# One order of work for a conditioned attention and gated-MLP block: mean-root products on either engine, statistics in two tasks, gates in bf16

## The chip, the cores and the metric

The kernel runs on one core of one Trainium2 chip. The core's engines run side by side, each through its own queue of instructions: TensorE (PE) multiplies matrices, with its weight loads shown as PEld, VectorE is DVE, ScalarE is ACT, GpSimd is POOL, and SyncE (SP) issues the transfers. Results of PE land in PSUM, everything else stands in SBUF. The metric is the device time of one execution in microseconds (us); lower is better. A profiled execution gives the trace from which the rows here come. A line such as L753 is a line of the kernel file.

## The reference, cut to what matters

One batch of 2048 tokens of 512 numbers goes through two residual branches. A vector `c` gives six rows that shift, scale and gate the branches.

```python
mod = (silu(c) @ w_mod).reshape(1, 6, 1, 512)
sa, ca, ga, sb, cb, gb = mod[:, 0], ..., mod[:, 5]
h = layernorm(x) * (1 + ca) + sa
x = x + ga * A(h)
h = layernorm(x) * (1 + cb) + sb
x = x + gb * B(h)

def A(h):                       # 32 heads of 16
    q, k, v = split(h @ wqkv)
    pq, pk = q @ w_phi, k @ w_phi           # per head
    phi = lambda p: concat(softmax(p), softmax(-p))
    kv = phi(pk).T @ v;  z = sum over tokens of phi(pk)
    o = (phi(pq) @ kv) / (phi(pq) @ z + 1e-6)
    return o @ wo

def B(h):
    return (sigmoid(h @ w_gate) * (h @ w_up)) @ w_down    # inner width 1376
```

The sums `kv` and `z` run over all tokens. So no output of the attention (no numerator) can be formed before the keys and values of all 2048 tokens are through.

## The kernel before, in words

The 2048 tokens are 16 tiles of 128. The program is first written as a graph of some 1230 small tasks. Each task has a name, the engines it may run on, and the keys that it reads and writes. Then a long string, `ORDER`, lists every task once; the tasks are issued in that order, each to the queue of its engine. `name@A`, `@D` or `@P` puts a task on ACT, DVE or POOL; without a mark it goes to the first engine of its list. Within an engine, tasks run strictly in the order of the string; between engines, semaphores hold a task until what it reads is there. So the string alone decides what waits behind what. It was found by a planner that has a cost in us for each task and engine (the numbers in braces in the code, such as `{"DVE": 0.83}`), but these costs have no part in the running program.

The first stage, up to the first numerators (`num0a`), runs as follows.

- Loads: `ld_x...` bring x in pieces of 2 or 4 tiles, `ld_wk`, `ld_wv` the key and value weights, `ld_wm0...` the first shift and scale weights (two halves, 0 and 1), `ld_wmga` and `ld_wmm2` the other modulation weights, `wqT` transposed query weights, all on SyncE's queue.
- `c1`, `c2`, `c3` form silu(c). `modc1.0`, `modc1.1` multiply it with the first modulation weights, and `modc1c0`, `modc1c1` copy the shift and scale columns out of PSUM (L630 to L638). `modca` and `modc2` do the same for the first gate and for the rest.
- `tpw`, `wTc`, `fold`, `foldc` fold `w_phi` into the key weights (side 1) and query weights (side 0): transposes, copies, products, copies (L661 to L685).
- First layer norm: `st1_t` computes the statistics of tile t and then aggregates them to mean and variance (L702, L703), one task of two DVE instructions. `rs1_g` forms the root of a group of one or two tiles, on ACT (logarithm, exponential, L709) or POOL (L712). `nmr1_g` multiplies mean, root and -1, one small DVE instruction for each tile (L718). `xn1_t` normalizes a tile with root and product as scale and bias (L731; tile 0 on DVE at L729, without the product). `tph` transposes on PE (L744), and `hm1_gj` applies scale and shift to a quarter j of group g, on ACT or DVE (L751, L753). The tiles of groups 6 and 7 (tiles 10 to 13) are transposed by DMA instead (`xT1`).
- Per tile t: `K` and `V` (PE, L817, L821; some in halves a and b), `e` (two exponentials on ACT, L776), `n` (sums on DVE, L780), `r` (reciprocal on DVE, L798, or logarithm and exponential on ACT, L794), `phi` (product on POOL or DVE, L787), `va` (copy of v), and `kv` (PE, accumulates key-value sums, L282). Tiles 11, 13, 14, 15 are cut into parts (`e11.2` is the part from feature group 2).
- For seven query tiles: `Q`, `qe`, `qn`, `qphi`, `pT`, likewise, with the last a transpose by DMA.
- `kvn`, `kvz` mask the finished sums (DVE, L294, L299), and the numerators `num` begin.

The gates: `modcac` and `modc2c` write a gate to four columns of `gcol`. `gwa`, `gwb` store them to DRAM and `gra`, `grb` read them back as a row, spread over all 128 partitions (L843, L846), on SyncE's queue. `wo0` to `wo3` multiply the rows of the output weights by the first gate (L851), `wd0` to `wd10` those of the down weights by the second (L860), on POOL or DVE.

After the numerators the order goes on with division, output product, second layer norm and the MLP (`g`, `tg`, `u`, `hm`, `y`, `fin`, `st`).

```python
def arrange(self, text):
    ...
    for word in text.split():
        name, _, e = word.partition("@")
        t = self.tasks[name]
        t.eng = LETTER[e] if e else next(iter(t.alts))
        assert t.eng in t.alts and t.deps <= done and t not in done, name
...
G.add(f"rs1_{g}", {"ACT": 0.43, "POOL": 1.1}, f_rs, r=[("mv1", t) for t in ts], w=[("rs1", g)])
```

Of the kernel before, what the change touches and what calls it, by code (L numbers as in the profile page):

```python
# [8 lines left out]
FP32 = mybir.dt.float32  # L9
# [3 lines left out]
ALU = mybir.AluOpType  # L13
# [30 lines left out]
K1a hm1_20@A ld_x2a hm1_12 hm1_02@A wqT1 ld_x3a tph03 xn1_4 hm1_23 hm1_13@A tph41 st1_8 hm1_03@A hm1_41@A st1_9 K0a hm1_22@A rs1_6@P tph43 hm1_43@A tph40 K1b
rs1_5@P K0b ld_wv0 wqT3 tph30 tph33 tph32 K2a tph42 hm1_40 wqT2 fold01 hm1_33 tph31 nmr1_6 K2b ld_wmga st1_14 hm1_30@A xn1_11 e0.0 hm1_31@A wqT0 xn1_10 xT1_11
K3a xT1_10 K3b foldc01 nmr1_5 xn1_8 V3a st1_15 e3.0 V0a rs1_8@P e2.0 V0b V3b fold03 va3 foldc03 ld_wmm2 V2a st1_12 n0.0 V2b xn1_9 fold02 nmr1_8 r0.0@A hm1_32
modca.0 va0 foldc02 modca.1 tph50 n2.0 xn1_15 modcac hm1_50 n3.0 e1.0 xn1_14 phi0.0 hm1_60@P V1a V1b hm1_62@P K4a hm1_63@P fold00 tph82 tph52 K4b foldc00
# [113 lines left out]
def kernel(  # L161
# [535 lines left out]
    for g, ts in enumerate(LG):  # L697
        n = len(ts)
        xns = []
        for t in ts:  # L700
            def f_st(e, t=t):
                dve.bn_stats(st1[:, t, :], x_sb[:, t, :])  # L702
                dve.bn_aggr(mv1[:, t, :], st1[:, t, :])  # L703
            G.add(f"st1_{t}", {"DVE": 0.83}, f_st, r=[("x", t)], w=[("mv1", t)])
# [354 lines left out]
```

## Time and profile before

| what | value |
|---|---|
| median of 3 runs | 204.14 us (203.95 to 204.27) |
| the profiled execution | 204.01 us |
| its span, first to last instruction | 202.3 us |
| granted clock of PE | 1.00 |
| busy: PE, DVE, ACT, POOL | 195.3, 160.1, 105.1, 104.7 us |
| moved by DMA | 22.92 MB, mean 113 GB/s |

The span is what the trace covers; the execution's own time lies 1.7 us above it. Busy time counts an instruction from its start to its end; on one engine neighbours can overlap by some hundredths of a us, so a duration may be longer than the room that it takes. In rows of the timeline, "x2" merges neighbours of one kind, and a bracket tells how long the engine stood before the row and what released it. Matmul ends are modelled; their starts are measured.

### The profile page before, as it was taken

What the parts mean: (1) busy time and instruction counts of PE and PEld (TensorE: products, weight loads), DVE (VectorE), ACT (ScalarE), POOL (GpSimd) and SP (SyncE); (2) the same over time, 40 slices, a digit from 0 to 9 for tenths busy, and PEclk for the clock granted to TensorE, in tenths of its full rate; (3) what the DMA queues carried; (4) which work ended last, traced back from release to release, by engine and by line L of the source; (5) the groups of instructions that cost most, each with busy time, mean ns of one, the idle gap of its engine ahead of it and who ended that gap; (6) DMA issues with size and microseconds to landing.
All of it is one profiled execution on the core that took longest, in us unless ns stands there. A gap on an engine that the chain in (4) does not pass through costs nothing.

```text
span 202.3 us, 4156 instructions
## 1 busy us (share of the span) xinstructions
PE 195.3 (97%) x1471; PEld 106.1 (52%) x1471; DVE 160.1 (79%) x374; ACT 105.1 (52%) x253; POOL 104.7 (52%) x147
## 2 busy tenths in 40 slices
PE   7989999999999999999999999999999999999993
PEld 2555565455464787668844444444444444444442
DVE  3999989999999999998897796884969754326623
ACT  2899998999978985576441215212113320334100
POOL 4999987888699998866670066130030332000000
PEclk9999999999999999999999999999999999999999
DMA  5999956669973963418655233542113031000011
GB/s 169 326 293 236 282 213 122 111 57 241 393 281 74 136 103 59 80 34 102 129 78 80 54 76 82 104 105 52 26 26 81 2 78 52 30 3 20 33 55 55
DMA packets 49452, 22.92 MB, mean 113 GB/s; under 512 B 38065, under 2 KB 47634, under 8 KB 49426
## 3 DMA queue, kind: packets, MB, share of 16 engines
q1 hardware_dynamic: 48896, 22.59, 49.7%
q8 instruction: 12, 0.20, 0.4%
q14 instruction: 14, 0.11, 0.2%
q10 hardware_dynamic: 530, 0.02, 0.1%
HBM read 11.58 MB, written 2.10 MB: 68 GB/s over the span
## 4 chain that ended last, share of the span: by engine, by line
PE 74%; DVE 7%; DMA 6%; ACT 5%; SPq 3%; issue 2%; POOL 1%; POOLq 0%; DVEq 0%; ACTq 0%
PE y_ps L485 19%; PE u_ps L447 18%; PE g_ps L447 17%; DMA wmod_sb<-in_w_mod_dram 6%; PE a_ps L356 6%; PE k_ps L817 3%; PE v_ps L821 3%; PE num L326 2%; PE q_ps L871 2%; ACT e L776 2%; DVE ks L780 2%; PE g_ps L449 1%; DVE qks L780 1%; SPq L537 1%; DVE phi L787 1%
## 5 line engine op out<-in xcount | busy, mean ns | idle before, releaser
L457 ACT ACTIVATE tg<-g_ps 128x512 bf16<-128x512 f32 (+5 forms) x66 | 28.9, 455 | 66.8 <-PE g_ps L447 39.7
L485 PE MATMUL y_ps<-wd_sb,wmod_sb 128*128 128x512 bf16 (+4 forms) x187 | 45.7, 367 | 0.0
L468 DVE SCALAR_TENSOR_TENSOR wmod_sb<-tg,u_ps 128x512 bf16<-128x512 bf16 (+4 forms) x63 | 30.3, 491 | 18.0 <-ACT tg L457 11.5
L447 PEld LDWEIGHTS <-wg_sb 128*128 128x128 bf16 (+1 forms) x252 | 21.9, 99 | 16.1
L447 PEld LDWEIGHTS <-wu_sb 128*128 128x128 bf16 (+1 forms) x252 | 21.8, 99 | 15.9 <-issue 0.3
L784 POOL TENSOR_TENSOR qphi<-qe,qks 128x512 bf16<-128x512 bf16 x24 | 25.1, 1061 | 4.2 <-DMA pT<-qphi 1.6
L485 PEld LDWEIGHTS <-wmod_sb 128*128 128x128 bf16 (+1 forms) x187 | 17.0, 97 | 16.0 <-issue 0.6
L447 PE MATMUL u_ps<-wT_sb,wu_sb 128*128 128x512 bf16 (+2 forms) x124 | 23.8, 322 | 0.0
L447 PE MATMUL g_ps<-wT_sb,wg_sb 128*128 128x512 bf16 (+2 forms) x124 | 23.1, 322 | 0.0
L447 PE MATMUL g_ps<-wqk_sb,wg_sb 128*128 128x128 bf16 (+4 forms) x128 | 20.0, 287 | 0.0
L447 PE MATMUL u_ps<-wqk_sb,wu_sb 128*128 128x128 bf16 (+4 forms) x128 | 19.8, 287 | 0.1
L376 POOL TENSOR_SCALAR ve<-mv 128x2 f32<-128x2 f32 (+1 forms) x8 | 1.8, 224 | 33.7 <-DVE mv L366 33.6
L492 DVE TENSOR_TENSOR ot<-y_ps,x 128x512 bf16<-128x512 f32 (+2 forms) x17 | 11.1, 654 | 10.2 <-PE y_ps L485 10.1
L780 DVE TENSOR_REDUCE qks<-qe 128x64 bf16<-128x1024 bf16 x16 | 19.2, 1204 | 0.0
L780 DVE TENSOR_REDUCE ks<-e 128x64 f32<-128x1024 bf16 (+2 forms) x22 | 19.1, 899 | 0.0
L776 ACT ACTIVATE e<-k_ps 128x512 bf16<-128x512 f32 (+2 forms) x44 | 18.0, 514 | 0.0
L776 ACT ACTIVATE qe<-q_ps 128x512 bf16<-128x512 f32 x32 | 17.1, 613 | 0.6 <-POOL phi L787 0.3
L817 PE MATMUL k_ps<-wqk_f,h1T 128*128 128x512 bf16 x64 | 16.6, 379 | 0.0
L871 PE MATMUL q_ps<-wqk_f,h1T 128*128 128x512 bf16 x64 | 15.9, 378 | 0.4 <-ACT wqk_f L685 0.4
L356 PE MATMUL a_ps<-wo_sb,oT 128*128 128x512 bf16 x64 | 16.3, 379 | 0.0
L787 POOL TENSOR_TENSOR phi<-e,kr 128x1024 bf16<-128x1024 bf16 (+2 forms) x10 | 14.4, 1446 | 3.3 <-ACT kr L795 2.1
L821 PE MATMUL v_ps<-wv_sb,h1T 128*128 128x512 bf16 x64 | 15.8, 379 | 0.2 <-ACT vaug L836 0.2
(132 smaller groups left out, 307.4 us busy)
## 6 DMA issues: line engine op xcount, KB each, us to landing
out_dram<-ot SPq DMA_DIRECT2D x15, 128.0 KB, 1.8
x_sb<-in_A_x_dram SPq DMA_DIRECT2D x6, 256.0 KB, 4.7
wmod_sb<-in_w_mod_dram SPq DMA_DIRECT2D x1, 1536.0 KB, 6.9
wu_sb<-in_B_w_up_dram SPq DMA_DIRECT2D x1, 1376.0 KB, 11.3
wg_sb<-in_B_w_gate_dram SPq DMA_DIRECT2D x1, 1376.0 KB, 12.1
wd_sb<-in_B_w_down_dram SPq DMA_DIRECT2D x1, 1280.0 KB, 8.3
wmod_sb<-in_w_mod_dram SPq DMA_DIRECT2D x4, 256.0 KB, 6.1
wqk_sb<-in_A_wqkv_dram SPq DMA_DIRECT2D x2, 256.0 KB, 4.4
```

The costliest lines, as they stand in the source:

```text
L356: pe.matmul(ap_[:], lhsT=oT[:, j, :], rhs=wo_sb[:, j, :], start=(j == 0), stop=(j == KT - 1))
L447: pe.matmul(ps[:fsz, 0:n], lhsT=w[:, j, ft * P:ft * P + fsz], rhs=h[:, j, 0:n], start=(j == 0), stop=(j == KT - 1))
L457: G.add(f"tg{k}.{ft}", {"ACT": 0.13 + n * 0.00083}, lambda e, tg=tg, g_ps=g_ps, fsz=fsz, n=n: act.activation(tg[:fsz, 0:n], g_ps[:fsz, 0:n ...
L468: dve.scalar_tensor_tensor(hm_all[:fsz, hm[k].slot, ft, 0:n], tg[:fsz, 0:n], 1.0, u_ps[:fsz, 0:n], op0=ALU.add, op1=ALU.mult)
L485: mm = pe.matmul(y[:, 0:c1 - c0], lhsT=hm_all[:fsz, hm[k].slot, ft, tl * P:(tl + 1) * P], rhs=wd_sb[:fsz, ft, c0:c1], start=(ft == 0), sto ...
L776: act.activation(ee[:, a:b, s].rearrange("p g f h -> p g (f h)"), kp[:, a * 64:b * 64].rearrange("p (g n) -> p g n", n=64), ACT.Exp, scale ...
L780: dve.tensor_reduce(ks[:, a:b].rearrange("p g s h -> p (g s) h"), ee[:, a:b].rearrange("p g s f h -> p (g s) h f"), axis=AX.X, op=ALU.add)
L784: engine(e).tensor_tensor(ph[:].rearrange("p (g s f h) -> p g s f h", s=2, f=DH, h=4)[:, :, s], ee[:, :, s], ks[:, :, 1 - s].unsqueeze(2). ...
L787: engine(e).tensor_tensor(ph[:, a * P:b * P].rearrange("p (g f h) -> p g f h", f=DH, h=4), ee[:, a:b].rearrange("p g s f h -> p (g s) f h" ...
L817: pe.matmul(kp[:], lhsT=h1T[:, j, t * P:(t + 1) * P], rhs=wqk_f[:, j, D:2 * D], start=(j == 0), stop=(j == KT - 1))
L821: pe.matmul(vp[:], lhsT=h1T[:, j, t * P:(t + 1) * P], rhs=wv_sb[:, j, :], start=(j == 0), stop=(j == KT - 1))
L871: pe.matmul(qp[:], lhsT=h1T[:, j, t * P:(t + 1) * P], rhs=wqk_f[:, j, 0:D], start=(j == 0), stop=(j == KT - 1))
```

## The change: what it does

Three edits in the tasks, and a new order for the first stage. From `num0a` to the end the string is the same, word for word; the sizes, splits and constants are the same too.

1. `nmr1_g` may run on POOL as well as DVE. In the new order all eight (15 instructions) run on POOL.
2. `st1_t` becomes two tasks, `st1s_t` (statistics) and `st1a_t` (aggregate), so that other work can stand between them.
3. The gate columns, their DRAM rows and the spread gate rows are bf16 instead of float32, so the products with `wo` and `wd` read bf16 only, and the spread rows are 1 KB for each partition instead of 2 KB.

Engines that change in the new order (groups and tiles as above):

| from, to | tasks |
|---|---|
| DVE to POOL | nmr1_1 to nmr1_8; qphi2.0, qphi2.1, qphi4.1; phi11.0, phi11.2, phi11.4 |
| ACT to DVE | r1, r2, r3, r4, r6, r9, r10; hm1_00, 03, 10, 11, 20, 21, 30, 31, 42, 82; foldc00; wTc3; modc1c0 |
| DVE to ACT | hm1_12, 23, 32, 40, 50, 52, 81, 83; va2 |
| POOL to DVE | qphi0.0, qphi0.1, qphi1.0, qphi1.1; wo1 |
| POOL to ACT | rs1_0, rs1_4, rs1_6; xn1_7; hm1_60 |

The loads come as x1b, x0a, x0b, wk1, wk0, x1a, x2b, then the four wm0 pieces (before: x0b, x0a, wk0, x1b, wk1, x1a, two wm0 pieces, x2b, two wm0 pieces). The first statistics are of tiles 7, 6, 0, 1, 2, 3, 4, 11, 5, 10 (before: 3, 2, 1, 0, 6, 7, 5, 4). The first key product is of tile 3 (before: tile 1). `mask4`, a small reduction on DVE that `kvn` and `kvz` need, goes to the very start. `gwa`, `gwb` and `gra` stand further ahead of the large weight loads. The diff, cut to its core:

```diff
 ORDER = """
-wdz warm0 c1 warm1_0 warm1_1 warm1_2 warm1_3 warm1_4 ld_x0b st1_3 st1_2 rs1_2 pmem ld_x0a c2 st1_1 ld_wk0 nmr1_2 tpw1 c3 rs1_1 ld_x1b wTc1 nmr1_1 st1_0 ld_wk1
...
+wdz ld_x1b warm0 c1 ld_x0a mask4 pmem c2 bd st1s_7 st1s_6 st1s_0 ld_x0b st1a_7 warm1_0 st1a_6 warm1_1 warm1_2 warm1_3 warm1_4 warm1_5 ld_wk1 warm1_6 rs1_4
+nmr1_4@P warm1_7 st1a_0 rs1_0 st1s_1 xn1_6 tpw2 st1s_2 st1a_1 warm1_8 tpw3 ld_wk0 rs1_1 c3 st1a_2 st1s_3 warm1_9 nmr1_1@P ld_x1a tpw1 tpw0 xn1_1 xn1_7@A tph40
+ld_x2b xn1_0 tph00 st1a_3 wTc3@D wTc2 rs1_2 nmr1_2@P wTc1 fold13 tph11 st1s_4 st1a_4 st1s_11 tph10 ld_wm00b fold11 st1s_5 xn1_3 warm1_10 warm1_11 wTc0 fold10
+st1a_11 foldc13 ld_wm00a xn1_2 st1a_5 foldc11 fold12 ld_wm01a rs1_3@P modc1.0 foldc10 st1s_10 tph41 tph21 modc1c0@D ld_wm01b foldc12 hm1_11 tph23 tph42 hm1_00
+hm1_40@A nmr1_3@P tph20 hm1_10 st1a_10 tph43 hm1_20 hm1_41@A tph01 hm1_01@A hm1_21 ld_x2a modc1.1 tph03 rs1_6 tph22 modc1c1@D hm1_22@A tph02 xn1_4 hm1_03 K3a
...
-    gb_bc = wmod_sb[:].rearrange("p k n -> p (k n)")[:, 2 * FT * 512:].bitcast(FP32)
+    gb_bc = wmod_sb[:].rearrange("p k n -> p (k n)")[:, 2 * FT * 512:2 * FT * 512 + D]
...
-    ga_sb = cst.tile([P, D], FP32, name="ga_sb")
+    ga_sb = cst.tile([P, D], BF16, name="ga_sb")
...
-    gcol = cst.tile([P, 8], FP32, name="gcol")
-    gdr = [drp.tile([P, KT], FP32, name=f"gdr{i}") for i in range(2)]
+    gcol = cst.tile([P, 8], BF16, name="gcol")
+    gdr = [drp.tile([P, KT], BF16, name=f"gdr{i}") for i in range(2)]
...
-            def f_st(e, t=t):
-                dve.bn_stats(st1[:, t, :], x_sb[:, t, :])
-                dve.bn_aggr(mv1[:, t, :], st1[:, t, :])
-            G.add(f"st1_{t}", {"DVE": 0.83}, f_st, r=[("x", t)], w=[("mv1", t)])
+            G.add(f"st1s_{t}", {"DVE": 0.66}, lambda e, t=t: dve.bn_stats(st1[:, t, :], x_sb[:, t, :]), r=[("x", t)], w=[("st1", t)])
+            G.add(f"st1a_{t}", {"DVE": 0.18}, lambda e, t=t: dve.bn_aggr(mv1[:, t, :], st1[:, t, :]), r=[("st1", t)], w=[("mv1", t)])
...
-                    dve.tensor_scalar(nmr[:, 0, t:t + 1], mv1[:, t, 0:1], rs1[:, t:t + 1], -1.0, op0=ALU.mult, op1=ALU.mult)
-            G.add(f"nmr1_{g}", {"DVE": 0.02 + 0.1 * n}, f_nm,
+                    engine(e).tensor_scalar(nmr[:, 0, t:t + 1], mv1[:, t, 0:1], rs1[:, t:t + 1], -1.0, op0=ALU.mult, op1=ALU.mult)
+            G.add(f"nmr1_{g}", {"DVE": 0.02 + 0.1 * n, "POOL": 0.3 * n}, f_nm,
```

More of the change, by code (lines that the diff above doesn't have):

```diff
@@ L44 @@
[L44 to L47, printed above, removed]
```

77 lines of the change are left out of this document (39 added, 38 removed).

## The prediction

> **What bounds the kernel now.** The page first, for the shares of the span.
> ```profile
> span 202.3 us, 4156 instructions
> PE 195.3 (97%) x1471; PEld 106.1 (52%) x1471; DVE 160.1 (79%) x374; ACT 105.1 (52%) x253; POOL 104.7 (52%) x147
> ```
> TensorE (PE) looks like the only limit, but the share is an average. So the same counts by stage next; columns are the stretch, its length, then busy us of PE, PEld, DVE, ACT and POOL, the granted clock and DMA.
> ```profile
> 3.72:12.66 8.94, 7.78 (x78) 4.45 (x78) 8.55 (x28) 6.90 (x20) 6.92 (x12) 1.00 1.19 312
> 12.66:28.85 16.19, 15.69 (x179) 9.44 (x179) 15.28 (x39) 16.00 (x42) 15.43 (x23) 1.00 1.10 273
> 28.85:38.86 10.01, 9.84 (x83) 5.24 (x81) 9.97 (x16) 9.45 (x25) 8.09 (x10) 1.00 0.55 105
> 38.86:57.51 18.65, 18.29 (x161) 9.64 (x160) 18.55 (x39) 17.90 (x57) 15.31 (x13) 1.00 0.89 235
> 57.51:73.00 15.49, 15.35 (x176) 10.40 (x177) 14.89 (x44) 13.36 (x33) 15.25 (x17) 1.00 0.61 118
> 73.00:199.00 126.00, 125.93 (x801) 66.21 (x798) 92.32 (x212) 40.24 (x84) 41.40 (x58) 1.00 0.32 62
> ```
> The first numerators start at 57.51. Ahead of that VectorE (DVE) is as full as PE: 8.55 + 15.28 + 9.97 + 18.55 = 52.35 us busy of 53.79, and in the last 28.66 us it idles 0.14 in all. After 73 only PE is full, and its work is the same in both kernels. The chain of waits says who ends the first stage:
> ```profile
> 55.73 1.13 DVE qks L780
> 56.86 0.37 DVE kvb L294
> 57.51 0.93 PE num L326 x24
> ```
> DVE finishes a reduction, masks the key-value sums, and PE goes on. So I treat everything after 57.51 as a fixed 144.8 us and ask when the numerators start, which is a question of how much work DVE has ahead of them.
>
> **The prices.** Vector instructions overlap, so I price each by its start to the start of the next in DVE's timeline, not by its duration.
> ```profile
> 4.45 0.18 DVE L703 BATCH_NORM_AGGREGATE mv<-st 128x2 f32<-128x6 f32 x1
> 4.55 0.66 DVE L702 BATCH_NORM_STATS2 st<-x_sb 128x6 f32<-128x512 bf16 x1
> 5.24 0.18 DVE L703 BATCH_NORM_AGGREGATE mv<-st 128x2 f32<-128x6 f32 x1
> ...
> 13.32 0.15 DVE L638 TENSOR_TENSOR modc<-modc_ps,mone 128x4 f32<-128x4 f32 x1
> 13.51 0.67 DVE L753 TENSOR_SCALAR h1T<-tp_h,modc 128x128 bf16<-128x128 bf16 x2
> 14.09 0.69 DVE L702 BATCH_NORM_STATS2 st<-x_sb 128x6 f32<-128x512 bf16 x1
> ...
> 23.59 0.68 DVE L836 CAST vaug<-v_ps 128x512 bf16<-128x512 f32 x1
> 24.19 0.68 DVE L702 BATCH_NORM_STATS2 st<-x_sb 128x6 f32<-128x512 bf16 x1
> ...
> 28.00 0.33 DVE L718 TENSOR_SCALAR nmr<-mv,rs 128x1 f32<-128x1 f32 x2 [0.60 <-POOL rs L713]
> 28.25 0.68 DVE L787 TENSOR_TENSOR phi<-e,kr 128x1024 bf16<-128x1024 bf16 x1
> ...
> 32.55 0.75 DVE L784 TENSOR_TENSOR qphi<-qe,qks 128x512 bf16<-128x512 bf16 x2
> 33.22 1.21 DVE L780 TENSOR_REDUCE ks<-e 128x64 f32<-128x1024 bf16 x1
> ...
> 37.66 0.28 DVE L591 TENSOR_REDUCE mask<-ident 128x4 bf16<-128x128 bf16 x1
> 37.85 0.40 DVE L753 TENSOR_SCALAR h1T<-tp_h,modc 128x256 bf16<-128x256 bf16 x1
> 38.17 0.54 DVE L798 RECIPROCAL kr<-ks 128x64 bf16<-128x64 f32 x1
> 38.63 0.31 DVE L753 TENSOR_SCALAR h1T<-tp_h,modc 128x256 bf16<-128x256 bf16 x1
> ...
> 49.91 1.36 DVE L787 TENSOR_TENSOR phi<-e,kr 128x256 bf16<-128x256 bf16 x4
> 51.19 1.27 DVE L780 TENSOR_REDUCE ks<-e 128x32 f32<-128x512 bf16 x2
> ```
> Read off: a reciprocal 0.46 (38.17 to 38.63), a 256-wide modulation 0.32 (37.85 to 38.17), a 128-wide one 0.26 (13.51 to 14.09 holds one of each), the shift-and-scale copy 0.19, a 512-wide copy out of PSUM 0.60 (23.59 to 24.19), a query product 0.335 (two in 32.55 to 33.22), a mean-root product 0.12 (two in 28.00 to 28.25), the mask 0.19. In 49.91 to 51.19 three quarter-width key products stand beside one full one; with 0.60 for the full one a quarter costs 0.23.
>
> **Onto DVE.** Seven reciprocals that ScalarE (ACT) did as a logarithm and an exponential (tiles 1, 2, 3, 4, 6, 9, 10): 7 x 0.46 = 3.22. Ten modulations of the first layer norm: 4 x 0.26 + 6 x 0.32 = 2.96. A fold copy 0.60. A copy of transposed weights (bf16 in PSUM, no such row on DVE): between 0.32, half as many elements, and 0.60, float32; I take 0.45. The shift-and-scale copy 0.19. Query products, four in and three out: 0.335. One wo product with a bf16 gate: between 0.335 (the query product, all bf16) and 0.60; I take 0.335. Sum 8.1 us.
>
> **Off DVE.** Fifteen mean-root products: 1.8. Eight modulations: 0.26 + 7 x 0.32 = 2.5. One v copy 0.60. Three quarter key products 0.7. The mask goes to the time before the first x lands, which is idle: 0.19. Sum 5.8 us.
>
> **Statistics in two tasks.** No instruction is removed. Now the aggregate waits for its own statistics: 4.55 to 5.24 is 0.69, then 0.10 more. The new order puts another instruction between the two for 15 of 16 tiles. A neighbour of the same duration that nothing waits for, the copy at 23.59, gives way after 0.60, 0.08 before its end. So a pair falls from 0.79 to about 0.70: 15 x 0.10 = 1.5 us; bounds 0 and 1.8. The Trainium skill ("VectorE: DVE Perf Modes", "The DRAIN you can't avoid") says that after every Vector operation the next does not start until the pipe is empty, and that this can't be skipped by leaving waits out; by that alone the split would be worth nothing. The rows at 4.45 and 4.55 disagree: statistics start 0.08 before the aggregate ends.
>
> **The sum.** +8.1 - 5.8 - 1.5 = +0.8 us of DVE work. Against it goes the 0.60 wait at 28.00, where DVE stood for a GpSimd (POOL) root: that product is POOL's own now, behind the root on the same engine, and DVE waits for it no more. Net +0.2. What is late next is DVE itself, since the other engines get lighter:
>
> ACT and POOL, with their rows:
> ```profile
> 10.71 0.21 ACT L635 COPY modc<-modc_ps 128x2 f32<-128x2 f32 x1
> ...
> 24.09 0.31 ACT L794 ACTIVATE ks<-ks 128x64 f32<-128x64 f32 x1
> ...
> 24.59 0.57 ACT L836 CAST vaug<-v_ps 128x512 bf16<-128x512 f32 x1
> ```
> ```profile
> 15.18 0.22 POOL L712 TENSOR_SCALAR ve<-mv 128x2 f32<-128x2 f32 x1
> 26.14 0.73 POOL L712 TENSOR_SCALAR ve<-mv 128x2 f32<-128x2 f32 x1
> 56.60 3.40 POOL L851 TENSOR_TENSOR wo_sb<-wo_sb,ga_sb 128x512 bf16<-128x512 bf16 x3
> 59.96 2.06 POOL L784 TENSOR_TENSOR qphi<-qe,qks 128x512 bf16<-128x512 bf16 x2
> ```
> ACT loses seven pairs of 0.50 (24.09 to 24.59), 3.5 us; of the rest it gives up twelve larger instructions and takes eleven and three root pairs, about +0.9 together (an estimate from the same pair). So it is 2 to 3 us lighter, and over the whole stage the exponentials that DVE reduces need come no later. On POOL the mean-root products cost 15 x 0.22 = 3.3, at most 15 x 0.73 where DVE multiplies beside them as at 26.14; I take the low end, because DVE runs statistics in that stretch. Queued behind each are the normalized tiles that PE transposes. POOL gives up three roots, a normalized tile, a modulation, a query product and a wo product, so its stage total falls too.
>
> **Gates in bf16.** Three wo and eleven wd products stay on POOL: 1.12 each (56.60 to 59.96), 1.03 if they run like the all-bf16 query products, 14 x 0.09 = 1.3 us. None of it has PE behind it: among the waits that PE's matmuls had from 4 to 100 us, five in all, none is for POOL. Two of the five, and the row transfer:
> ```profile
> PE modc_ps L630 <- DMA wmod_sb<-in_w_mod_dram: 0.6, 1, 0.6
> ...
> PE num L326 <- DVE kvb L299: 0.4, 1, 0.4
> ```
> ```profile
> ga_sb<-gdr SPq DMA_DIRECT2D x1, 256.0 KB, 5.0
> ```
> The transfer shrinks to 128 KB and is queued earlier, and so are the large weights that stand behind the two gate rows on SyncE's queue. The first wo product ran on POOL right behind a key product, without a wait for the row; so what was hidden before stays hidden: worth 0. If the row came 5.0 us later than I think, it would still land ahead of the last key products. Halved gate writes likewise cost nothing.
>
> **PE and the loads.** PE's work is the same. Its first key product starts here:
> ```profile
> 13.19 0.59 PE L817 MATMUL k_ps<-wqk_f,h1T 128*128 128x512 bf16 x2
> ```
> The loads up to the second half of the first modulation are the same bytes in another order. But the first shift-and-scale copy, at 10.71 on ACT, now stands on DVE behind ten statistics (one of them with its aggregate right behind), nine aggregates and three small steps of about 0.4 (an estimate after the copies above): 3.72 + 10 x 0.60 + 0.1 + 9 x 0.1 + 3 x 0.4, about 11.9. The modulations that the first key product needs follow to 13.6, so PE starts its keys 0.2 to 0.5 late. It has that to spare, as DVE sets the stage's end.
>
> **Forecast: 204.3 us.** The profiled execution took 204.01 for its span of 202.3, 0.13 under the median of 204.14. Change +0.2: 204.2 for that execution, 204.3 beside the median. A change under 0.2% (0.41 us) can't be told from none.
>
> **The rivals.** *DVE runs without any wait* (faster). For it: the open prices may all lie low. Weight copy 0.32 instead of 0.45, split 1.8 instead of 1.5, and the remaining small idle times (52.35 busy of 53.79 leaves 0.8 beside the 0.60) half gone: -0.13 - 0.3 - 0.4 against +0.2, so -0.6, 203.5. Against: DVE has more work, not less. Chance 0.27.
>
> *The late first modulations reach DVE* (slower). Place: 13 to 22 us. From a start of the keys after about 13.8, the first exponentials come after DVE is through its statistics, and DVE stands idle, which it can't make up. For it: by the sum above DVE gets to its first key reduction at about 20 and its second at 21.3, and ACT, its queue begun 1.2 us late, delivers the second exponential at about 21. Price: the 0.6 wait returns here instead of going, 204.9. Against: ACT's lighter load. Chance 0.27.
>
> *The split is worth nothing.* If an aggregate between strangers waits as long as before, +1.5: 205.8. The overlapped rows speak against it. Chance 0.06. The Trainium skill's rule for the pipe ("VectorE: DVE Perf Modes", as above) would come out here.
>
> *The change doesn't do what it says* would be the bf16 row not shortening POOL's products; that costs nothing either way.
>
> **Numbers.** Forecast 0.40, faster rival 0.27, the two slower ones 0.33. The range leaves out the split rival and the outer parts of the others: 203.4 to 205.4; the likeliest case alone 203.9 to 204.7.
>
> **What would show it.** Right: the numerators start at 57.5 to 57.9, DVE idle under 0.5 us from 3.7 to there, statistics start to start near 0.60, no DVE wait for a POOL root, ACT with over 2 us idle in the stage, 144.8 us from numerators to the end. Wrong: DVE waits for ACT before 25 us, statistics still 0.69, or a later stretch whose length differs by more than 0.3 us, which would mean the gates or the earlier loads matter after all.

## The result, and the profile after

The changed kernel takes 206.23 us (median of 5 runs, 205.70 to 207.56), and before, on the same chip, 204.05 us (5 runs, 203.95 to 204.27). The ratio is 1.0111, with a 95% interval of 1.0074 to 1.0147: slower by 1.1%, where 204.3 was forecast and 205.4 was the upper end of the range. The profiled execution took 206.23 us, 1.7 above its span, as before. Executions with a lower granted clock take longer (the changed kernel: 205.70 to 206.24 us at 1.00, 207.56 at 0.992), and one each of e11 and e12, at 0.75 and 0.855, is left out below, with it the only profile of e12.

The head of the page after, then the same windows as in the prediction (busy us of PE, PEld, DVE, ACT and POOL, then granted clock and DMA):

```profile
span 204.5 us, 4127 instructions
...
PE 195.1 (95%) x1447; PEld 106.8 (52%) x1471; DVE 162.8 (80%) x369; ACT 103.6 (51%) x242; POOL 105.1 (51%) x155
```
```profile
3.72:12.66 8.94, 8.36 (x78) 4.78 (x78) 8.38 (x27) 6.29 (x18) 6.81 (x13) 1.00 1.12 318
12.66:28.85 16.19, 16.03 (x154) 9.64 (x156) 16.02 (x36) 16.13 (x39) 15.07 (x28) 1.00 1.20 275
28.85:38.86 10.01, 9.96 (x112) 5.76 (x110) 9.98 (x14) 10.01 (x25) 8.34 (x10) 1.00 0.58 107
38.86:57.51 18.65, 17.17 (x136) 8.60 (x137) 18.30 (x34) 16.61 (x50) 15.80 (x15) 1.00 0.89 250
73.00:199.00 126.00, 125.21 (x808) 67.01 (x821) 92.80 (x217) 42.12 (x90) 43.49 (x60) 1.00 0.33 62
```

Up to 38.86 PE is busier than before (34.35 against 33.31 us in the three rows together). In the row from 38.86 on PE has 1.1 us less than before (17.17 against 18.29), while DVE is busy for 18.30 of 18.65 us. But with what? The chain of waits of the changed kernel names it (start, us, what):

```profile
49.68 1.15 DVE phi L786
...
55.61 2.43 DVE phi L786 x2
58.03 1.13 DVE qks L779
...
59.63 1.02 PE num L327 x24
```

The numerators start at 59.63 instead of 57.51, 2.12 us late; from there to the end it takes 144.87 us, before 144.77. The whole loss lies ahead of the numerators, and at the end of that stage two half-width key products (`phi13.0`, `phi15.0`) take 2.43 us on DVE.

The timelines of DVE and POOL show why. DVE after, then POOL after (start, duration; the bracket is the time the engine stood before and what released it):

```profile
49.68 1.15 DVE L786 TENSOR_TENSOR phi<-e,kr 128x1024 bf16<-128x1024 bf16 x1
...
53.92 0.62 DVE L786 TENSOR_TENSOR phi<-e,kr 128x1024 bf16<-128x1024 bf16 x1
...
55.53 2.50 DVE L786 TENSOR_TENSOR phi<-e,kr 128x512 bf16<-128x512 bf16 x2
```
```profile
48.52 1.76 POOL L786 TENSOR_TENSOR phi<-e,kr 128x256 bf16<-128x256 bf16 x3 [0.26 <-ACT vaug L835]
50.91 2.06 POOL L786 TENSOR_TENSOR phi<-e,kr 128x512 bf16<-128x512 bf16 x2 [0.62 <-DVE phi L786]
54.23 2.22 POOL L786 TENSOR_TENSOR phi<-e,kr 128x512 bf16<-128x512 bf16 x2 [1.26 <-DVE kr L797]
56.41 3.75 POOL L850 TENSOR_TENSOR wo_sb<-wo_sb,ga_sb 128x512 bf16<-128x512 bf16 x3
```

The same two engines before, at the last key products:

```profile
54.43 1.29 DVE L787 TENSOR_TENSOR phi<-e,kr 128x512 bf16<-128x512 bf16 x3
```
```profile
52.15 2.05 POOL L787 TENSOR_TENSOR phi<-e,kr 128x512 bf16<-128x512 bf16 x2
55.49 1.15 POOL L787 TENSOR_TENSOR phi<-e,kr 128x512 bf16<-128x512 bf16 x1 [1.28 <-ACT kr L795]
```

Before, three products (two half ones and a full one) take 1.29 us on DVE, and they stand in a stretch in which POOL waits 1.28 us for a reciprocal. After, POOL has none of that idle time at that place: the second product of its row at 54.23 starts at 55.41 and runs to 56.45, and `phi13.0` starts on DVE at 55.53, 0.12 us later. It takes 1.21 us where 0.36 was its time before. Then POOL takes its next product (56.41) before DVE takes its own (56.66), and `phi15.0` takes 1.37 us where it had taken 0.41. Likewise `phi10.0` at 49.68 stands on DVE behind the last quarter product of POOL (49.67 to 50.29) and takes 1.15 us, 0.68 before. By the room from start to start the three take 1.07, 1.13 and 1.30 us instead of 0.60, 0.28 and 0.33: 2.29 us more, against a loss of 2.12.

A product of DVE and one of POOL thus exclude each other: who comes second waits until the other's instruction is all but over. It goes both ways: the first product in POOL's row at 54.23 runs beside a DVE product that began at 53.92 and takes 1.21 us; 1.05 is what it takes alone. DVE's mask products, which have one input in PSUM, are not held: at 59.17 each takes 0.41 us beside a POOL product, 0.42 to 0.43 before. The Trainium skill ("SBUF — State Buffer", "Who interferes with whom") says that a VectorE instruction with two inputs in SBUF contends with a GpSimd instruction that reads SBUF, that the shared ports are an exclusive lock, that the order of issue decides who is blocked, and that on trn2 `tensor_reduce` never contends. The trace agrees: the reduction that DVE runs at 47.06, beside a POOL product, takes 1.16 us, and 1.15 to 1.22 is what such reductions take elsewhere. Only where the two recorded starts lie within 0.04 us do they not tell who is first: DVE waits at 49.68 in the changed kernel (POOL starts 0.01 us ahead) and is free at 55.44 in e3 below (0.02 ahead).

A second, smaller thing: ACT waited 1.42 us for an exponential's buffer, which the transpose `pT1` still read. That transpose stood on SyncE's queue for 3.58 us, behind the store of the second gate, which the new order had put ahead of it. ACT's row, then SyncE's (SyncE is written SPq):

```profile
42.94 2.66 ACT L775 ACTIVATE e<-k_ps 128x128 bf16<-128x128 f32 x10 [1.42 <-DMA pT<-qphi]
```
```profile
36.45 0.53 SPq L842 DMA_DIRECT2D gdr<-gcol  x1
37.91 3.58 SPq L873 DMA_TRANSPOSE pT<-qphi  x1
```

DVE lost 0.32 us by it, at 45.6. Two theories came out of this. **P**: the loss is DVE's products blocked by POOL's. **L**: the loss is DVE fed late by ACT, the gate store among its causes, and the long products only fill time that would be idle. A third, **E**: the edits themselves cost DVE more than was worked out.

### The profile page after: what moved, and what is told of

It reads as the page before. It is cut to its first block, busy times and chain, and to the rows that moved or that the text cites. A ratio compares the mean times of both kernels' runs of the same rounds, so it can differ in the third digit from the quotient of the medians.

```text
span 204.5 us, 4127 instructions
## 1 busy us (share of the span) xinstructions
PE 195.1 (95%) x1447; PEld 106.8 (52%) x1471; DVE 162.8 (80%) x369; ACT 103.6 (51%) x242; POOL 105.1 (51%) x155
## 4 chain that ended last, share of the span: by engine, by line
PE 76%; ACT 8%; DVE 8%; DMA 4%; issue 2%; DVEq 0%; ACTq 0%
PE y_ps L486 18%; PE u_ps L448 17%; PE g_ps L448 17%; PE a_ps L357 6%; PE q_ps L870 3%; PE k_ps L816 3%; DMA pT<-qphi 2%; DVE ks L779 2%; ACT e L775 2%; PE num L327 2%; DVE phi L786 2%; PE v_ps L820 2%; ACT qe L775 2%; PE tp_h L743 2%; DVE st L702 1%
## 5 line engine op out<-in xcount | busy, mean ns | idle before, releaser
L486 PE MATMUL y_ps<-wd_sb,wmod_sb 128*128 128x512 bf16 (+4 forms) x180 | 44.2, 366 | 0.2
L783 POOL TENSOR_TENSOR qphi<-qe,qks 128x512 bf16<-128x512 bf16 x23 | 23.9, 1056 | 5.0 <-DMA pT<-qphi 1.7
L775 ACT ACTIVATE e<-k_ps 128x512 bf16<-128x512 f32 (+2 forms) x44 | 19.1, 570 | 1.5 <-DMA pT<-qphi 1.4
L786 POOL TENSOR_TENSOR phi<-e,kr 128x1024 bf16<-128x1024 bf16 (+2 forms) x13 | 16.4, 1280 | 3.7 <-DVE kr L797 1.3
L816 PE MATMUL k_ps<-wqk_f,h1T 128*128 128x512 bf16 x60 | 15.6, 379 | 0.2
```

Of the source, the lines that this page charges most:

```text
L486: mm = pe.matmul(y[:, 0:c1 - c0], lhsT=hm_all[:fsz, hm[k].slot, ft, tl * P:(tl + 1) * P], rhs=wd_sb[:fsz, ft, c0:c1], start=(ft == 0), sto ...
L775: act.activation(ee[:, a:b, s].rearrange("p g f h -> p g (f h)"), kp[:, a * 64:b * 64].rearrange("p (g n) -> p g n", n=64), ACT.Exp, scale ...
L783: engine(e).tensor_tensor(ph[:].rearrange("p (g s f h) -> p g s f h", s=2, f=DH, h=4)[:, :, s], ee[:, :, s], ks[:, :, 1 - s].unsqueeze(2). ...
L786: engine(e).tensor_tensor(ph[:, a * P:b * P].rearrange("p (g f h) -> p g f h", f=DH, h=4), ee[:, a:b].rearrange("p g s f h -> p (g s) f h" ...
L816: pe.matmul(kp[:], lhsT=h1T[:, j, t * P:(t + 1) * P], rhs=wqk_f[:, j, D:2 * D], start=(j == 0), stop=(j == KT - 1))
```

## The experiments

Before was run beside all of them: 203.95 us (23 runs) beside e1 to e4, 203.93 (23) beside e5 to e8, 203.88 (16) beside e9 to e11, 203.78 (11) beside e12. The changed kernel was run only for the result above, so a comparison with it goes across sessions. All starts of the numerators in one place; "blocked" counts DVE products of 1.1 us or more in the last 10 us ahead of them:

| kernel | median us | ratio to before (95%) | numerators at | to the end | blocked |
|---|---|---|---|---|---|
| before | 204.05 | 1 | 57.51 | 144.8 | 0 |
| after | 206.23 | 1.0111 (1.0074 to 1.0147) | 59.63 | 144.9 | 3 |
| e1, edits on the old order | 204.56 | 1.0021 (0.9994 to 1.0049) | 58.87 | 144.7 | 1 |
| e2, before with one POOL product earlier | 207.53 | 1.0166 (1.0120 to 1.0212) | 60.02 | 145.6 | 3 |
| e3, after with two POOL products earlier | 204.88 | 1.0029 (1.0003 to 1.0054) | 58.57 | 144.8 | 2 |
| e4, after with the gate store later | 205.73 | 1.0102 (1.0056 to 1.0148) | 59.37 | 144.5 | 3 |
| e5, after with POOL out of the way | 204.36 | 1.0015 (0.9997 to 1.0032) | 57.78 | 144.9 | 0 |
| e6, e5 with mean-root products on DVE | 211.30 | 1.0357 (1.0337 to 1.0378) | 64.81 | 144.6 | 0 |
| e7, e5 with two reciprocals on ACT | 204.19 | 1.0008 (0.9992 to 1.0024) | 57.16 | 145.1 | 0 |
| e8, after with float32 gates | 207.11 | 1.0141 (1.0110 to 1.0171) | 59.89 | 145.9 | 3 |
| e9, e1 with mean-root products on POOL | 210.42 | 1.0313 (1.0281 to 1.0346) | 63.23 | 145.3 | 1 |
| e10, e1 with the statistics apart | 204.64 | 1.0036 (1.0018 to 1.0054) | 58.25 | 144.5 | 1 |
| e11, e9 and e10 together, `wo1` on DVE | 210.47 | 1.0317 (1.0281 to 1.0354) | 63.33 | 145.3 | 0 |
| e12, e7 with a third reciprocal on ACT | 205.23 | 1.0060 (1.0040 to 1.0079) | not read | | |

**e2: only the collision, put into the kernel before.** One word moves, and no engine gets more or less work:

```diff
-Q5 phi15.4 phi13.0@D va15 phi15.0@D phi12.0@D wo0 wo3
+Q5 wo0 phi15.4 phi13.0@D va15 phi15.0@D phi12.0@D wo3
```

> The kernel before with one token moved: wo0 stands ahead of phi15.4 in POOL's queue, so POOL multiplies in the 1.3 us in which it was idle while DVE did phi13, phi15 and phi12. Theory P expects DVE's products there to wait for POOL's instruction to end: 0.9 us if one collides, 1.9 if two do, so the numerators at 58.4 to 59.4 and 204.9 to 206.0, and these products with durations over 1 us in place of 0.36 to 0.69. Theory L (the numerators are late because the exponentials reach DVE late) and theory E expect no change, 203.9 to 204.4, or a slight gain since the wo products end earlier.

DVE of e2, then POOL:

```profile
54.33 3.96 DVE L787 TENSOR_TENSOR phi<-e,kr 128x512 bf16<-128x512 bf16 x3
```
```profile
54.05 1.17 POOL L851 TENSOR_TENSOR wo_sb<-wo_sb,ga_sb 128x512 bf16<-128x512 bf16 x1
55.39 1.05 POOL L787 TENSOR_TENSOR phi<-e,kr 128x512 bf16<-128x512 bf16 x1 [0.17 <-ACT kr L795]
56.39 2.92 POOL L851 TENSOR_TENSOR wo_sb<-wo_sb,ga_sb 128x512 bf16<-128x512 bf16 x2
```

The three products that took 1.29 us now take 3.96. `wo0` fills POOL's 1.28 us of idle time, and from then on the engines alternate: each time DVE starts, POOL has begun an instruction shortly before. The numerators come 2.5 us late: theory P's mechanism is shown by itself. The size was missed: one to two blocked products were expected, three came.

The median is 3.6 us above before, but not all of that is the collision. In the profiled execution PE's granted clock falls to 0.50 for 3.4 us, from 58.95 on, so that this row (as in the result) has 0.89 where before has 1.00:

```profile
57.51:73.00 15.49, 14.51 (x144) 9.10 (x145) 14.60 (x37) 10.68 (x23) 11.30 (x12) 0.89 0.43 101
```

Five of e2's six executions have a mean clock of 0.984 to 0.992; the sixth, at 0.999, takes 206.33 us, 2.4 above before. So the collision by itself is worth 2.4 to 2.5 us. Whether PE's wait ahead of it (0.02 us busy from 56 to 58) brings the lower clock on is not shown; some executions of before have it too.

**e3: two POOL products out of the way in the changed kernel.**

```diff
-phi11.2 phi14.0
+phi11.2 wo0 phi14.0
...
-wmod_free phi13.4
+wmod_free wo3 phi13.4
...
-kv15.0 wo3 kv13.4 wo0 kvz0
+kv15.0 kv13.4 kvz0
```

> The changed kernel with wo0 moved ahead of phi14.0 and wo3 ahead of phi13.4 in POOL's queue, where DVE does sums. Theory P expects phi15 on DVE to lose its wait behind wo3 (about 1.0 us), with phi13 still waiting for POOL's phi15.4: numerators near 58.7, 205.2 to 205.6. Theory L expects 206.0 to 206.5, unchanged.

DVE, then POOL:

```profile
55.44 1.54 DVE L785 TENSOR_TENSOR phi<-e,kr 128x512 bf16<-128x512 bf16 x2
```
```profile
53.73 1.73 POOL L849 TENSOR_TENSOR wo_sb<-wo_sb,ga_sb 128x512 bf16<-128x512 bf16 x1
55.42 2.46 POOL L785 TENSOR_TENSOR phi<-e,kr 128x512 bf16<-128x512 bf16 x2
```

`phi13.0` and `phi15.0`, 2.50 us in the changed kernel, take 1.54: the first is free (0.36 us; POOL's product of 55.42 starts within 0.02 us of it and is the one that waits, so that its row of two takes 2.46 instead of 2.05), the second waits behind that product. One product freed brings the numerators 1.06 us forward and the time 1.35 us down, to 204.88, below the 205.2 to 205.6 that theory P gave; it had expected `phi15.0` to be the free one and `phi13.0` to wait.

**e4: the gate store behind the transpose.**

```diff
-e7.0 gwb r6.0 phi5.0 pT1 K14
+e7.0 r6.0 phi5.0 pT1 gwb K14
```

> The changed kernel with the store of the second gate row moved behind the transpose pT1 in SyncE's queue. In the changed kernel pT1 stood 3.6 us in the queue behind that store, and ACT waited 1.4 us at 42.9 for its buffer. Theory L expects that wait and DVE's 0.3 us at 45.3 to go and the numerators to come 0.3 to 1 us earlier, 205.2 to 205.9. Theory P expects ACT's wait to go but most of the gain to be lost again in the collisions at the end: 205.7 to 206.2.

ACT's wait for the transpose and DVE's idle time at 45.6 are gone, the three products stay blocked, and the numerators come at 59.37, 0.26 earlier. The time, 205.73, lies in the ranges of both theories, so it does not decide between them. What e4 shows is the store's part, 0.3 us at the numerators: with DVE's wait for ACT gone, 1.9 of the 2.1 us are still there.

**e1: the three edits with before's order.** Each `st1_t` becomes `st1s_t st1a_t` side by side; the mean-root products stay on DVE.

> The three edits in the tasks (bf16 gates, statistics as two tasks, mean-root product allowed on either engine) with the old order of work: each aggregate stands right behind its statistics and the mean-root products stay on DVE. Theory P (in the new order DVE's two-input products collide with POOL's at the end of the stage) expects no change from before, 203.7 to 204.4, numerators at 57.3 to 57.7, because the edits alone move nothing. Theory E (an edit in itself costs time, for instance the bf16 rows) expects 205 or more.

The edits alone take 204.56 us, 0.6 above before and 0.2 above theory P's range; the interval still holds a ratio of 1. The profiled execution took 205.28, so its numerators (58.87, where theory P gave 57.3 to 57.7) are later than those of a median one. Of the 1.36 us that they are late, rows of DVE, then POOL:

```profile
11.78 0.33 DVE L716 TENSOR_SCALAR nmr<-mv,rs 128x1 f32<-128x1 f32 x2 [0.61 <-POOL rs L711]
...
50.45 2.19 DVE L785 TENSOR_TENSOR phi<-e,kr 128x256 bf16<-128x256 bf16 x4
```
```profile
50.41 1.27 POOL L849 TENSOR_TENSOR wo_sb<-wo_sb,ga_sb 128x512 bf16<-128x512 bf16 x1 [0.88 <-DMA ga_sb<-gdr]
```

0.61 is a wait for POOL's root at 11.78, and it belongs to this execution: the weights for `bd`, POOL's first product, land at 5.81 us, where 4.6 to 5.1 stands in the other profiles. 0.83 is a product blocked in the row at 50.45 (2.19 us; 1.36 before): the gate row lands late, POOL starts `wo1` 0.88 us late, and so in front of DVE. Again a meeting on the port, made by a transfer.

That lateness comes from the bf16 edit. The gate's store to DRAM lands later although it is half as large, and the read waits for it. The store of the second gate before, then in e1 (KB each, us from issue to landing):

```profile
gdr<-gcol SPq DMA_DIRECT2D x2, 2.0 KB, 5.3
```
```profile
gdr<-gcol SPq DMA_DIRECT2D x2, 1.0 KB, 7.1
```

For the first gate, whose store is issued at 41.6 in both, the read follows after 1.9 us before and after 3.3 in e1. The other runs of this order have the same: 1.7 and 4.9 us in e2 with float32, 2.9 to 3.3 and 7.1 to 7.6 in e9 to e11 with bf16. Why the smaller store takes longer is open. So theory E is right in this much: with before's order the bf16 edit brings one blocked product, 0.8 us. The 2 us of DVE work that it named are not there.

**e5: all of the collisions removed.** `phi11.2` and `phi15.4` go to DVE, `wo0` into POOL's idle time ahead of `phi13.4`, `wo3` and `wo2` behind the first query product, which POOL can't start before DVE is past its key products:

```diff
-e7.0 gwb r6.0 phi5.0 pT1
+e7.0 r6.0 phi5.0 pT1 gwb
...
-phi10.0@D
+phi11.2@D phi10.0@D
...
-phi11.2 phi14.0
+phi14.0
...
-phi13.4
+wo0 phi13.4
...
-kv15.0 wo3 kv13.4 wo0 kvz0
+kv15.0 kv13.4 kvz0
...
-phi15.4 phi13.0@D Q5 phi15.0@D
+phi13.0@D Q5 phi15.0@D phi15.4@D
...
-num2a wo2
+num2a qphi6.0@P wo3 wo2
...
-Q8 qphi6.0@P qphi6.1@P
+Q8 qphi6.1@P
```

> The changed kernel with POOL's products taken out of the way of DVE's: key product phi11.2 and phi15.4 go to DVE, wo0 goes into POOL's gap ahead of phi13.4, wo3 and wo2 stand behind the first query product, and the second gate store stands behind the transpose pT1. Theory P (DVE products blocked by POOL products): phi10, phi13 and phi15 fall back to about 0.68, 0.36 and 0.41 us (together 2.3 us less), two products of 0.20 and 0.33 are added, the 0.3 us gap at 45.6 goes: numerators at 59.63 - 2.35 + 0.53 - 0.31 = 57.5 us, 204.0 us in all. Theory L (late exponentials feed DVE late): only the 0.3 goes, numerators at 59.3 or later, 205.9 or more. Theory E (the edits themselves cost 2 us of DVE): numerators stay near 59, 205.5 or more.

DVE, then POOL:

```profile
47.87 0.68 DVE L849 TENSOR_TENSOR wo_sb<-wo_sb,ga_sb 128x512 bf16<-128x512 bf16 x1
...
55.16 1.02 DVE L785 TENSOR_TENSOR phi<-e,kr 128x512 bf16<-128x512 bf16 x3
56.11 1.21 DVE L778 TENSOR_REDUCE qks<-qe 128x64 bf16<-128x1024 bf16 x1
```
```profile
53.87 1.22 POOL L785 TENSOR_TENSOR phi<-e,kr 128x512 bf16<-128x512 bf16 x1 [0.36 <-ACT qe L774]
57.48 1.05 POOL L782 TENSOR_TENSOR qphi<-qe,qks 128x512 bf16<-128x512 bf16 x1 [2.40 <-DVE qks L778]
```

The last three key products take 1.02 us together, and POOL stands 2.40 us meanwhile. The numerators come at 57.78, 1.85 us ahead of the changed kernel, though DVE has two products more (0.53 us). The 0.28 us that are missing to the 57.5 of theory P are `wo1`: at 47.87 it is still behind a POOL product and takes 0.68 us instead of the 0.36 that it took in the changed kernel. DVE has no idle time at all from 43 us to the numerators. The time is 204.36 us, where theory L gave 205.9 or more and theory E 205.5 or more: both fall here. The loss of the change is the collisions and the 0.3 us of the gate store, and without them the change makes no difference that can be told from none.

**e7: two reciprocals back on ACT.**

```diff
-r9.0 ... r10.0
+r9.0@A ... r10.0@A
```

> e5_clear with the reciprocals r9.0 and r10.0 (0.41 us each on DVE) back on ACT as a logarithm and an exponential, about 0.5 us there. Theory P: DVE is the bound once the collisions are gone and ACT has 2 us to spare between 39 and 57.5 us: numerators 0.8 us ahead of e5_clear, near 56.7, 203.2 us. Theory L: ACT feeds DVE late, so two more pairs on ACT gain nothing or lose up to 1 us.

The numerators come 0.62 us ahead of e5, most of the 0.8 expected; the rest went to `phi11.2`, whose pair with `phi10.0` takes 1.17 us where 0.87 stood in e5, again beside a POOL product. So DVE is the bound in this execution once more. The median doesn't bear it out: 204.19 us is 0.17 below e5, which can't be told from none, and 1.0 above what theory P gave. From the numerators to the end this execution took 145.1 us, 0.2 more than e5's. Why the rest of the 0.62 doesn't reach the median is open.

**e12: a third reciprocal on ACT and `wo1` behind the last key product.**

```diff
-r8.0 ... wo1@D ... va15 kv13.0 qn6.0
+r8.0@A ... va15 kv13.0 wo1@D qn6.0
```

> e7_clear_roots with a third reciprocal, r8.0 (0.46 us on DVE), back on ACT, and wo1 on DVE moved behind the last key product, where POOL has nothing under way, so that it should take 0.28 instead of the 0.61 us that its row shows in e5_clear and e7_clear_roots. Theory P (DVE has no gap in e7_clear_roots from 43 us to the numerators, so each instruction shortened or taken off counts): 0.33 + 0.46 = 0.8 us ahead of e7_clear_roots at the numerators, 56.4 us, about 203.4 us. Rival (ACT, 17.67 of 18.65 us busy there, is full with the third pair and feeds DVE late): DVE shows gaps again, numerators at 57 us or later, 204.2 us.

205.23 us, 1 us slower than e7, against the theory, and 1 us above what the rival gave. Two edits are in it and no usable trace, so that ACT was full is argued, not shown. No version here beats before.

**e6: the mean-root products on DVE again, in e5's order.**

```diff
-nmr1_4@P ... nmr1_1@P ... nmr1_2@P ... nmr1_3@P ... nmr1_6@P ... nmr1_5@P ... nmr1_8@P ... nmr1_7@P
+nmr1_4 ... nmr1_1 ... nmr1_2 ... nmr1_3 ... nmr1_6 ... nmr1_5 ... nmr1_8 ... nmr1_7
```

> e5_clear with the 15 mean-root products of group 1 and later back on DVE. My theory: 15 x 0.12 = 1.8 us come back onto DVE, and where one stands right behind its root DVE waits for that, 0 to 1 us more: numerators 1.8 to 2.8 us later than in e5_clear, 205.8 to 206.8 us. Rival (the products on POOL delay the normalised tiles and that is what DVE pays for): no later than e5_clear, 204.0 us or less.

7.0 us later at the numerators, not 1.8 to 2.8: a miss for both. DVE's waits up to 58 us, then POOL's longest (us in total, times, longest):

```profile
DVE phi L785 <- POOL phi L785: 2.5, 1, 2.5
...
DVE nmr L716 <- POOL rs L711: 1.4, 1, 1.4
DVE nmr L716 <- ACT rs L708: 1.0, 2, 0.7
```
```profile
POOL xn L729 <- DVE nmr L716: 11.4, 7, 3.7
```

The order places each product right behind its root. On POOL that costs little, since POOL makes the root or the tile behind it. On DVE 2.4 us of waiting for roots stand in front of modulations and reductions, and POOL's normalised tiles wait 11.4 us for DVE's products, a wait that e5 doesn't have. What those feed comes late (PE's first key product at 15.29, 13.92 in e5), and later DVE stands 2.5 us for a POOL product. The clock, 0.50 for 3.4 us in the profiled execution, is not the cause: an execution at 1.00 takes 210.72 us. So the edit and its order belong together, and the 1.8 us can't be read from this kernel.

**e9, e10, e11: the other way about, on before's order.** On e1, the products on POOL (e9); the aggregate behind the next DVE instruction for 12 of 16 tiles (e10); both, and `wo1` on DVE (e11).

```diff
-nmr1_2 ... nmr1_1 ... nmr1_4 ... nmr1_3 ... nmr1_6 ... nmr1_5 ... nmr1_8 ... nmr1_7
+nmr1_2@P ... nmr1_1@P ... nmr1_4@P ... nmr1_3@P ... nmr1_6@P ... nmr1_5@P ... nmr1_8@P ... nmr1_7@P
```
```diff
-st1s_3 st1a_3 st1s_2 st1a_2 rs1_2
+st1s_3 st1s_2 st1a_3 st1a_2 rs1_2
...
```

> Before's order with the three edits to the tasks (as e1_edits_old_order, 204.56 us, first numerators 58.87) and the 15 mean-root products on POOL, nothing else. My theory (each DVE instruction taken off counts in full, as DVE is the bound ahead of the numerators): 15 x 0.12 = 1.8 us off DVE and the 0.6 us wait at 28 gone, numerators at 56.5 to 57.5 us, 202.3 to 203.3 us, unless a key product meets a POOL product at the shifted times: each such meeting costs 0.5 to 1.0 us and its row on DVE shows 1.1 us or more. Rival (DVE is fed late): DVE waits longer elsewhere instead, numerators within 0.4 us of 58.87 with a DVE wait of 1 us or more on ACT or PE.

> Before's order with the three edits and each tile's closing task put behind the next DVE instruction where its root allows it (12 of 16 tiles), mean-root products still on DVE. My theory: an apart pair takes 0.67 instead of 0.79 us, so 12 x 0.12 = 1.4 us off DVE, minus what the roots wait longer for a closing that stands one instruction later: numerators 0.8 to 1.4 us ahead of 58.87, 203.2 to 203.8 us, again unless products meet. Rival (the page's rule that each dependent pair pays no matter what stands between): pair slots stay 0.79, 204.6 us.

> Both of the above on before's order, with the product wo1 on DVE (0.28 us) so that POOL has one product less among the key products. My theory: 1.8 + 1.4 + 0.6 - 0.3 = 3.5 us off DVE against e1_edits_old_order if nothing else ends later; PE's keys and ACT's exponentials then bind, so I expect numerators at 56.0 to 57.2 us, 201.8 to 203.2 us, faster than both kernels. Rival (products meet at the shifted times): two or three rows of 1.1 us or more on DVE, numerators at 57.5 to 59 us, 203.5 to 205 us.

e9 loses 6 us instead of gaining 1 to 2. POOL's first rows in e9:

```profile
6.04 0.49 POOL L716 TENSOR_SCALAR nmr<-mv,rs 128x1 f32<-128x1 f32 x2 [2.93 <-ACT c_ps L576]
...
6.98 1.49 POOL L580 TENSOR_TENSOR bd<-wp_sb,bmask 128x256 bf16<-128x256 bf16 x2
```

In before's order the first mean-root product stands ahead of `bd`, which the folds need. POOL waits 2.93 us for that product's root (the row names the ACT instruction right behind the root, which ends 0.07 us later), and `bd`, which had started at 4.97, starts at 6.98. The normalised tiles of POOL come late after it (PE waits 2.5 us for them up to 30 us), and PE's first key product starts at 14.87, where before has 13.19. How the rest of the loss adds up was not followed row by row. e11 shares it: 210.47 us, where both its theories gave 205 or less. The new order has `bd` among its first words. Neither theory had looked at POOL's queue behind the moved step.

e10 shows the numerators 0.62 us ahead of e1, under the 0.8 to 1.4 expected, but e1's profiled execution was 0.7 us slower than its median, so this can't be read as a gain. The median doesn't move: 204.64 after 204.56. The pairs do get shorter (0.66 us from 8.23 to 8.89, not the rival's 0.79), and part of it is lost in waits for roots that now get their aggregate one instruction later (0.5 us at 11.20, below). e10 has the same blocked product as e1, behind POOL's `wo1`; in e11, with `wo1` on DVE, the four products of that row take 1.23 us, and none is blocked.

```profile
3.64 1.29 DVE L701 BATCH_NORM_STATS2 st<-x_sb 128x6 f32<-128x512 bf16 x2 [2.45 <-DMA x_sb<-in_A_x_dram]
4.84 0.30 DVE L702 BATCH_NORM_AGGREGATE mv<-st 128x2 f32<-128x6 f32 x2
...
11.20 0.33 DVE L716 TENSOR_SCALAR nmr<-mv,rs 128x1 f32<-128x1 f32 x2 [0.52 <-POOL rs L711]
```

**e8: float32 gates in the changed kernel.** Columns, DRAM rows and spread rows are float32 again.

```diff
-    ga_sb = cst.tile([P, D], BF16, name="ga_sb")
+    ga_sb = cst.tile([P, D], FP32, name="ga_sb")
...
-    gcol = cst.tile([P, 8], BF16, name="gcol")
+    gcol = cst.tile([P, 8], FP32, name="gcol")
...
```

> The changed kernel with the gate rows, columns and their DRAM copies in float32 again, nothing else. My theory: the products of the output weight on POOL keep 1.1 us each, wo1 on DVE takes 0.3 to 0.7 us in place of 0.28, the gate row's transfer 5.0 in place of 4.6: 206.2 to 206.7 us, no more than 0.5 us either way. Rival (bf16 gates are what costs): faster than the changed kernel by 1 us or more.

The median, 207.11 us, is 0.9 above the changed kernel, more than the 0.5 allowed for, but the clocks differ. e8 takes 205.99, 206.10 and 206.72 us at a granted clock of 1.00 and 207.51 to 207.75 at 0.992; the changed kernel takes 205.70 to 206.24 at 1.00 and 207.56 at 0.992. At the same clock no difference can be told. The profiled execution is one at 0.992, and its low clock lies behind the numerators, hence 145.9 us from there to the end:

```profile
57.51:73.00 15.49, 13.51 (x116) 8.13 (x119) 14.10 (x35) 10.00 (x22) 11.92 (x12) 0.89 0.31 59
```

So bf16 gates neither gain nor cost in this kernel, and the rival is out. The products on POOL take the same: three in 3.77 us, 3.75 with bf16. On DVE `wo1` is dearer:

```profile
47.97 0.95 DVE L850 TENSOR_TENSOR wo_sb<-wo_sb,ga_sb 128x512 bf16<-128x512 bf16 x1
```

0.95 us instead of 0.36, but up to 0.4 of it is waiting: here a POOL product ran from 47.76 to 48.37, and none in the changed kernel. So float32 alone costs 0.2 to 0.6 there. The store goes the other way, as in e1: `pT1` stands 2.82 us behind the float32 store instead of 3.58, ACT waits 0.60 us for it instead of 1.42, and DVE's 0.32 us of idle time at 45.6 is gone. 0.59 more and 0.32 less make the 0.26 us by which the numerators are later.

## Why the prediction was wrong, point by point

**The step that failed** is the sum, where it says that "what is late next is DVE itself" and prices each DVE instruction by its row in before. The key products kept 0.60, 0.28 and 0.33 us in it, whatever POOL ran at their new places. For three of them these became 1.07, 1.13 and 1.30. The prediction had the clue in hand: it took a POOL row of 0.73 us (at 26.14, against 0.22) as the price "where DVE multiplies beside them", for POOL only. That the same lock stops DVE, and that before's order leaves POOL idle for just the 1.28 us in which DVE multiplies last, it didn't look at, though the trace of before has the row with this idle time (55.49, above). No rival had this mechanism, so the range couldn't hold it.

**All other terms came out well.** Below is the room on DVE from 3.7 us to the last query reduction (start of an instruction to start of the next, less idle time; for the statistics with the waits inside a pair), summed by kind:

| kind | before, us | after, us | change | forecast |
|---|---|---|---|---|
| statistics and aggregates | 12.88 | 11.16 | -1.7 | -1.5 |
| mean-root products | 1.77 | 0 | -1.8 | -1.8 |
| reciprocals, full width | 0.92 | 4.07 | +3.2 | +3.2 |
| modulations | 2.72 | 3.14 | +0.4 | +0.5 |
| copies, shift and scale | 0.75 | 1.24 | +0.5 | +0.6 |
| query products, `wo1` | 1.01 | 1.56 | +0.6 | +0.7 |
| quarter key products, mask | 0.88 | 0 | -0.9 | -0.9 |
| full and half key products | 5.01 | 6.93 | +1.9 | 0 |

Without the last row the work grows by 0.3 us, where 0.8 was forecast. 59.63 less the 1.9 of that row is 57.7, and 57.5 to 57.9 was forecast for the numerators. e5 comes near that case, though with two key products more on DVE: 204.36 us, 0.4 above the before run beside it, where +0.2 was forecast.

**The split** was mis-sized only a little: statistics keep the room of 0.58 to 0.61 us that was forecast, but for one pair left together (0.72). The changed kernel's first rows on DVE:

```profile
3.85 1.88 DVE L702 BATCH_NORM_STATS2 st<-x_sb 128x6 f32<-128x512 bf16 x3 [2.13 <-DMA x_sb<-in_A_x_dram]
5.64 0.30 DVE L703 BATCH_NORM_AGGREGATE mv<-st 128x2 f32<-128x6 f32 x3
```

Three statistics in 1.79 us and three aggregates in 0.22 make 0.67 for a pair, where 0.79 stood before. The Trainium skill ("VectorE: DVE Perf Modes", "The DRAIN you can't avoid"), whose rule for the pipe the prediction set against this, also says in that section that a next operation which is not held starts earlier. The rows agree with that: neighbours that don't depend on each other overlap by 0.08 us, and only a dependent pair loses that.

**The wait for POOL's root** at 28 is gone, as said. The mean-root products take 0.25 us each on POOL, 0.22 forecast. **ACT** is 1.2 us lighter over the four windows up to 57.51 (49.04 us busy, 50.25 before), not 2 to 3; in the last of them it idles 2.0 us, and e7 shows that this can be used. **PE's keys** start at 13.90, 0.7 late where 0.2 to 0.5 was said; DVE is full behind them, so this cost nothing. Instead the wait at 42.94 came up: "queued earlier" was right for the gate row, but the transpose behind the second gate's store was not weighed, 0.3 us at the numerators. **The gate row's transfer** shrinks less than its bytes:

```profile
ga_sb<-gdr SPq DMA_DIRECT2D x1, 128.0 KB, 4.6
```

4.6 us instead of 5.0. "Halved gate writes likewise cost nothing" is wrong: the smaller stores take longer (e1, e8), and both the late gate row of e1 and most of ACT's wait at 42.94 hang on them. Gates worth 0 on POOL is right (1.11 us for a product, 1.12 before); on DVE they are worth 0.2 to 0.6 us for the one product, by e8. **The fixed 144.8** from the numerators to the end held (144.9). Of the rivals, DVE starving at 13 to 22 us did not happen, nor did the split fail.

## What to carry to other kernels

Before moving a product with two inputs in SBUF on VectorE, list what GpSimd runs at its new time, and price it with the rest of that GpSimd instruction: 0.5 to 1.0 us each here, and again for the next product if GpSimd has more queued. Idle time on GpSimd beside VectorE's products may be what keeps them short, so filling it (e2) can cost 2.4 us though no engine has more to do. A task that is moved to another in-order queue needs its place chosen anew: on GpSimd the same fifteen small products take 1.8 us off VectorE in one order and make the kernel 6 us slower in another. Before two medians are compared, look at the granted clock of each execution: in e8 it made 0.9 us that the edit didn't.

## What the runs showed of the hardware that wasn't expected

The blocking comes in chains. In e2 DVE met POOL at three successive products, since POOL, once let go, started its next instruction 0.04 to 0.27 us before DVE started its own; three products of 1.29 us took 3.96.

It isn't only products. In e9 the normalised tile that DVE makes with one input in SBUF took 0.87 us beside POOL's of the same kind (in e11 too), and 0.38 in before, where POOL ran nothing of that size. In the changed kernel, where the two start within 0.01 us, it is the other way about: DVE's takes 0.40 and POOL's 0.88 instead of 0.77. DVE of e9, then POOL:

```profile
11.00 0.87 DVE L727 TENSOR_SCALAR xn<-x_sb,mv,rs 128x512 bf16<-128x512 bf16 x1 [0.40 <-POOL rs L711]
```
```profile
10.96 0.77 POOL L729 TENSOR_SCALAR xn<-x_sb,rs,nmr 128x512 bf16<-128x512 bf16 x1
```

A store of 1 KB can hold up a transpose: `pT1` stood 3.58 us in SyncE's queue behind the second gate's store, and with the store behind it (e4) the numerators came 0.3 us earlier. And the store of half the size lands later: 7.1 us for a gate in bf16 on before's order, 5.3 in float32.

PE's granted clock can halve for a short stretch: 3.4 us each in the profiles of e2, e6, e8 and e11. Executions of before with a mean clock of 0.992 take 205.0 to 205.5 us, about 1.3 more than its median beside e1 to e4.
